# Seven probability tiles taken once and used in turn, in a fused attention and feed-forward kernel: what the writers of a tile wait for

## The chip, the cores and the metric

The kernel runs on one core of one Trainium2 chip. The time is the device time of one execution in microseconds (us); it is given as the median of three runs. Beside it stands one profiled execution, whose hardware trace is what the profile's views are made from. The engines of the core are named as the profile names them: PE (matrix products; PEld is its loading of weights), DVE (vector), ACT (activations), POOL, and SP, which issues most of the transfers.

## The reference

The input is one sequence of 2048 tokens of width 512. Two branches are computed and mixed by a gate per token.

```python
g = sigmoid((x * gate_w).sum(-1))
q = (x @ wq)  -> 32 heads of 16        k = x @ wk, v = x @ wv   # one key and value head for all
p = softmax(q k^T * 16**-0.5)
a = (p v, heads side by side) @ wo
b = (silu(x @ w_gate) * (x @ w_up)) @ w_down                    # width 1792
out = g * a + (1 - g) * b
```

## The kernel before

**Numbers.** Products are made in a fast 32-bit format; to keep accuracy each factor is split into a high and a low part and three products are added (`split`, `three`). Queries carry high and low parts in 48 rows of a 64-row half, so that a score product is one matmul of 64 rows, and two of them stand side by side in the array. The products of the projections and of the feed-forward branch ("jobs", line 198) are also cut into halves of 64 rows; PE runs a lower half of one job beside the upper half of an earlier one.

**Attention.** Keys lie on the 128 partitions. For head h and key tile kt (16 of them), numbered together u = 16 h + kt, `score(u, j)` makes the scores of 128 keys against 1024 queries (j = 0 or 1) in a PSUM tile `pss` of two banks (line 741, two matmuls). There are two `pss` buffers, so a score product needs the one that the score product two before it used. `exps` turns scores into probabilities on ACT (line 749), into the probability tile `pt[u]`, 128 x 2048 numbers. There are two kinds of score tile. Kind A: ACT takes all 1024 columns out of PSUM. Kind H, "half": ACT takes the first 512 columns, DVE copies the other 512 raw into `pt` (line 745), and ACT makes their exponentials later in place (line 749, `pt<-pt`). `mix(u)` multiplies `pt[u]` by the values and by a column of ones (line 761, `po`), 32 rows at a time, four products side by side.

**Blocks.** After a first stage (u below 32, in pairs, all of kind A, with the last projections of the queries between), the rest runs in 120 blocks of four key tiles. A table writes the order out by hand: `STEPS` = "SSFFFFFSFSFFFSFFFSFFFFSS" (S a score product, F a step of feed-forward work on PE), then the four `mix`. `KINDS` = "AHHAAHHA" names the kinds of the eight score tiles of a block, here called tile 0 to tile 7, and `EXPS` = "0d 1d 2d 3d 4d 5d 5s 1s 2s | 6d T 7d 6s" is ACT's order (d straight from PSUM, s in place, T a tanh of the feed-forward branch). The first of the 120 blocks has all tiles of kind A, the last one has fewer tiles.

**Probability tiles.** `new_pt(u)` takes a new `pt` tile for each u: three buffers (`PTB`) lie in one pool, four (`PTL`) in another that opens when the query weights are gone; from u = 33 on they are used in turn, so that a buffer comes back after seven key tiles. The framework that turns the program into instructions finds for each writer of a new tile who wrote and read the buffer's old content, and adds a wait for each engine whose work the writer's engine hasn't yet waited for. A wait is for a semaphore of the other engine, or of the engine itself. Where an instruction has one wait, it carries it; where it has two, the first is put into an instruction of its own, EVENT_SEMAPHORE, on the queue ahead of it.

`ACTS`, `DEFER`, `LATER` and `COPY` are lists of feed-forward and normalisation work for ACT and DVE, which the blocks hand out between the attention steps.

Of the kernel before, what the change touches and what calls it, by code (L numbers as in the profile page):

```python
# [8 lines left out]
F32 = mybir.dt.float32  # L9
# [9 lines left out]
P = 128  # L19
S = 2048  # L20
D = 512
H = 32
DH = 16
F = 1792
KD = D // P
NT = S // P
CH = 512
# [20 lines left out]
PTB = 3  # L48
# [3 lines left out]
PTL = 4  # L52
# [13 lines left out]
def tile_gated_mix(ctx, tc, x, wq, wk, wv, wo, w_gate, w_up, w_down, gate_w, out):  # L66
    nc = tc.nc
# [19 lines left out]
    vaug = cpool.tile([P, NT, 2 * DH], F32, name="vaug")  # L87
# [18 lines left out]
    ACC, PAIR = {}, []  # L106
# [21 lines left out]
    def run(queue, n):  # L128
        for _ in range(min(n, len(queue))):
            queue.pop(0)()  # L130
# [592 lines left out]
    with tc.tile_pool(name="bpool", bufs=2) as bp:  # L723
        PT = {}
# [2 lines left out]
            nc.sync.dma_start(new_qs(h).bitcast(F32), q_d[h])  # L727


        def new_pt(u):  # L730
            late = u > 2 * BEGIN and (u - 2 * BEGIN) % (PTB + PTL) >= PTB
            PT[u] = (PAIR[1] if late else bp).tile([P, S], F32, name="pt", bufs=PTL if late else PTB)

        def score(u, j, half=False):
            h, kt = divmod(u, NT)
            if j == 0:
                new_pt(u)
            ps = ps_s.tile([P, 2 * CH], F32, name="pss")
            for b in range(2):
                rows = slice(b * RT, (b + 1) * RT)  # L740
                nc.tensor.matmul(ps[:, b * CH:(b + 1) * CH], ks[rows, kt * P:(kt + 1) * P], QS[h][rows, j, :],  # L741
                                 start=True, stop=True)
            halves.clock += 1
            pt = PT[u][:, j * 2 * CH:(j + 1) * 2 * CH]
            other = nc.vector.tensor_copy(pt[:, CH:], ps[:, CH:]) if half else None  # L745
            return pt, ps, other

        def exps(pt, ps, other=None, w=slice(None)):
            ins = nc.scalar.activation(pt[:, w], ps[:, w], AF.Exp, scale=SCALE)  # L749
            if other is not None:  # L750
                tc.declare_no_dep(getattr(ins, "ins", ins), getattr(other, "ins", other), reason="another bank")

        def mix(u):
            h, kt = divmod(u, NT)
            pt = PT.pop(u)
            if kt == 0:
                run(COPY, 1)
                PO[:] = [ps_o.tile([P, CH], F32, name="po")]
            po = PO[0]
            for c in range(NCH):  # L760
                nc.tensor.matmul(po[c * 2 * DH:(c + 1) * 2 * DH, :], vaug[:, kt, :], pt[:, c * CH:(c + 1) * CH],  # L761
                                 start=(kt == 0), stop=(kt == NT - 1))
            if kt == NT - 1:

                osb = hp.tile([P, CH], F32, name="osb")
                rsb = hp.tile([P, CH], F32, name="rsb", bufs=1)

                def invert(i):
                    w = slice(i * P, (i + 1) * P)
                    nc.vector.reciprocal(rsb[:, w], rsb[:, w])  # L770

                def store():
                    nc.vector.tensor_tensor(osb, osb, rsb, ALU.mult)
                    for c in range(NCH):
                        nc.sync.dma_start(o_d[h * DH:(h + 1) * DH, c * CH:(c + 1) * CH],
                                          osb[c * 2 * DH:c * 2 * DH + DH, :])

                assert not LATER
                COPY.append(lambda: nc.vector.tensor_copy(osb, po))
                LATER.extend([(0.8, lambda: nc.vector.stream_shuffle(rsb, osb, [DH] * 2 * DH))] +  # L780
                             [(1.0, lambda i=i: invert(i)) for i in range(TC)] + [(0.8, store)])

        NU = H * NT
        SPANS, u = [], 2 * BEGIN
# [6 lines left out]
        def feed(k, more=True):  # L791
            for _ in range(k):
                if JOBS or halves.busy():
                    halves.step(more)

        def block(k, u0, size, first, last, steps, kinds, order):
            more = k < NB - STOP
            tiles = [(u, j) for u in range(first, last) for j in range(2)]
            order = list(order)
            made = []  # L800

            def emit():
                while order and order[0] != "|" and (order[0] == "T" or int(order[0][:-1]) < len(made)):
                    what = order.pop(0)
                    if what == "T":
                        run(ACTS, len(ACTS))
                        continue
                    i, how = int(what[:-1]), what[-1]
                    pt, ps, other = made[i]
                    if how == "s":  # L810
                        exps(pt, pt, w=slice(CH, None))
                    else:
                        exps(pt, ps, other, slice(0, CH) if kinds[i] == "H" else slice(None))

            for i, what in enumerate(steps):
                if what == "F":
                    if "S" in steps[i + 1:i + 3] and kinds[len(made):len(made) + 1] == "H":
                        HOLD.append(i)
                    feed(1, more)
                    HOLD.clear()  # L820
                elif len(made) < len(tiles):
                    made.append(score(*tiles[len(made)], kinds[len(made)] == "H"))
                    emit()
                    run(EVAC, len(EVAC))
                if len(made) > 4:
                    run(COPY, 1)
            if order:
                order.pop(0)
            run(ACTS, len(ACTS))
            emit()  # L830
            assert not order and len(made) == len(tiles)
            left = BUDGET * size / 4
            rest = len([v for v, _ in SPANS if v >= u0 and v // NT == u0 // NT])
            for _ in range(max(-(-len(LATER) // rest), 0 if DEFER else 2)):
                if LATER:
                    cost, f = LATER.pop(0)
                    left -= cost
                    f()
            for last in (False, True):
                kept = set()  # L840
                for item in list(DEFER):
                    n, cost, f = item
                    if n in kept or (n in FRESH) != last or cost > left:
                        kept.add(n)
                    else:
                        DEFER.remove(item)
                        left -= cost
                        f()
            FRESH.clear()
            for u in range(u0, u0 + size):  # L850
                mix(u)
            halves.clock += size * LONG // 2
# [7 lines left out]
        with tc.manual_schedule():  # L860
            for j in range(2):
                exps(*score(0, j))
            for n in range(BEGIN):
                quota = RATE
                u = 2 * n
                if n == 0:
                    feed(FIRST)
                exps(*score(u + 1, 0))
                if n == 0:
                    feed(quota - FIRST)  # L870
                exps(*score(u + 1, 1))
                feed(FIRST)
                exps(*score(u + 2, 0))
                feed(quota - FIRST)
                exps(*score(u + 2, 1))
                settle()
                mix(u)
                mix(u + 1)
                halves.clock += LONG
                run(COPY, 1)  # L880
                if LATER:
                    LATER.pop(0)[1]()
                if n == NT // 2 + 1:
                    load_head(2)
# [62 lines left out]
    with tc.If(rv != 0):  # L947
        with tc.tile_pool(name="gpool", bufs=2) as gp:
            with tc.For_i(0, H, 1) as h:
# [4 lines left out]
                for qt in range(NT):  # L954
# [3 lines left out]
                    for half in range(2):  # L958
                        ps = ps_s.tile([P, 2 * CH], F32, name="pss")
                        for j in range(2):  # L960
                            c = half * 2 + j
# [9 lines left out]
                    po = ps_o.tile([P, CH], F32, name="po")  # L971
                    for b in range(NT // TC):
                        pt = ps_f.tile([P, CH], F32, name="pf")
                        for i in range(TC):
                            kt = b * TC + i
# [3 lines left out]
                        for i in range(TC):  # L979
                            kt = b * TC + i  # L980
                            nc.tensor.matmul(po[:2 * DH, :P], vaug[:, kt, :], ptc[:, i * P:(i + 1) * P],
                                             start=(kt == 0), stop=(kt == NT - 1))
# [39 lines left out]
```

## Time and profile before

| | |
|---|---|
| median of three runs | 1346.02 us (1345.85 to 1346.98) |
| the profiled execution's own time | 1346.55 us |
| its span in the profile | 1344.5 us |
| busy in the span | PE 1331.0 us, ACT 1088.3, DVE 786.8, weight loads 779.0, POOL 225.1 |
| granted PE clock | 0.998 of full speed |

The span is the time from the first to the last instruction of the program in the trace; 2 us of the execution lie outside it. PE's busy time is a union of instructions whose ends are modelled, so a PE that is busy 99% may still lose time inside: what it loses is seen in the distance from the start of one matmul to the start of the next, in the view of the instructions in order of time.

### The profile page before, as it was taken

The numbers are of one execution on the slowest core, as the hardware profiler recorded it, in microseconds if no ns is written. First come the engines' busy times: TensorE is split into PE (matmuls) and PEld (weight loads), VectorE is DVE, ScalarE is ACT, GpSimd is POOL, SyncE is SP. The second block draws the span as 40 slices with busy tenths as digits, with TensorE's granted clock in tenths as the row PEclk, the third lists the DMA queues.
The fourth block names the chain that finished last, engine by engine and source line by source line (L and its number), as shares of the span: only waits on it lengthen the run. The fifth ranks groups of instructions, "written<-read, shape, count | busy, mean of one in ns | idle before, by whom it ended". The sixth has DMA issues, their size and how long they took to land.

```text
span 1344.5 us, 27205 instructions
## 1 busy us (share of the span) xinstructions
PE 1331.0 (99%) x10782; PEld 779.0 (58%) x10782; DVE 786.8 (59%) x1342; ACT 1088.3 (81%) x1596; POOL 225.1 (17%) x229
## 2 busy tenths in 40 slices
PE   9999999999999999999999999999999999999988
PEld 7655555555555555555555555555555555555677
DVE  4654566566565665666556666565555666566542
ACT  4578898889898888889888889888888889888501
POOL 6250231142141151142010000000000000001043
PEclk9999999999999999999999999999999999999999
DMA  8676021131144372263234342242231342242254
GB/s 285 210 241 218 20 65 41 40 98 36 52 129 141 107 240 91 68 218 104 83 123 146 121 136 68 67 154 76 65 107 62 127 130 66 68 161 91 83 191 151
DMA packets 102515, 157.35 MB, mean 117 GB/s; under 512 B 11888, under 2 KB 43376, under 8 KB 100720
## 3 DMA queue, kind: packets, MB, share of 16 engines
q1 hardware_dynamic: 100656, 155.36, 35.9%
q8 instruction: 88, 1.44, 0.5%
q10 hardware_dynamic: 1728, 0.20, 0.1%
q14 instruction: 43, 0.35, 0.1%
HBM read 99.42 MB, written 55.57 MB: 115 GB/s over the span
## 4 chain that ended last, share of the span: by engine, by line
PE 97%; DVE 2%; ACT 1%; issue 0%; DVEq 0%; ACTq 0%
PE pf L198 37%; PE po L761 34%; PE pss L741 21%; PE pf L120 4%; PE pss L627 0%; ACT pt L749 0%; DVE rsb L770 0%; PE po L614 0%; DVE hl L111 0%; DVE hh L110 0%; DVE xl L632 0%; PE pss L667 0%; DVE rsb L780 0%; DVE ht L337 0%; DVE pt L745 0%
## 5 line engine op out<-in xcount | busy, mean ns | idle before, releaser
L749 ACT ACTIVATE pt<-pss 128x1024 f32<-128x1024 f32 (+1 forms) x1024 | 783.0, 823 | 144.5 <-PE pss L741 125.3
L745 DVE COPY pt<-pss 128x512 f32<-128x512 f32 x475 | 328.1, 691 | 396.1 <-PE pss L741 391.6
L761 PE MATMUL po<-pt,vaug 128*32 128x512 f32 x4096 | 468.0, 595 | 0.0
L741 PE MATMUL pss<-qs,ks 64*128 64x512 f32 x2048 | 404.0, 423 | 1.4 <-DVE sign L484 1.0
L741 PEld LDWEIGHTS pss<-qs,ks 64*128 64x128 f32 x2048 | 192.4, 184 | 217.4 <-ACT pt L749 189.1
L749 ACT ACTIVATE pt<-pt 128x512 f32<-128x512 f32 x475 | 272.7, 621 | 17.5 <-DVE pt L745 10.7
L761 PEld LDWEIGHTS po<-pt,vaug 128*32 128x32 f32 x4096 | 131.3, 109 | 246.4 <-issue 222.3
L198 PE MATMUL pf<-xh,wgh 64*128 64x512 f32 (+1 forms) x444 | 164.9, 391 | 0.0
L198 PE MATMUL pf<-xh,wgl 64*128 64x512 f32 (+1 forms) x444 | 164.7, 390 | 0.0
L198 PE MATMUL pf<-xl,wgh 64*128 64x512 f32 (+1 forms) x444 | 164.2, 390 | 0.0
L198 PE MATMUL pf<-xh,wul 64*128 64x512 f32 (+1 forms) x440 | 160.7, 390 | 0.0
L198 PE MATMUL pf<-xh,wuh 64*128 64x512 f32 (+1 forms) x440 | 160.5, 390 | 0.1
L198 PE MATMUL pf<-xl,wuh 64*128 64x512 f32 (+1 forms) x440 | 160.1, 390 | 0.0
L198 PE MATMUL pf<-wdh,hh 64*128 64x512 f32 x416 | 136.2, 390 | 0.0
L198 PE MATMUL pf<-wdl,hh 64*128 64x512 f32 x416 | 135.0, 390 | 0.0
L198 PE MATMUL pf<-wdh,hl 64*128 64x512 f32 x416 | 134.6, 390 | 0.0
L770 DVE RECIPROCAL rsb<-rsb 128x128 f32<-128x128 f32 x128 | 116.7, 933 | 1.8 <-issue 0.8
L515 POOL CAST xh<-wraw 128x512 fp32r<-128x512 f32 x4 | 2.9, 727 | 513.2 <-DMA wraw<-o_d 513.2
L198 PEld LDWEIGHTS pf<-xl,wgh 64*128 64x128 f32 (+1 forms) x444 | 80.4, 185 | 8.2 <-issue 0.8
L198 PEld LDWEIGHTS pf<-xh,wgl 64*128 64x128 f32 (+1 forms) x444 | 80.6, 185 | 7.7
L198 PEld LDWEIGHTS pf<-xh,wgh 64*128 64x128 f32 (+1 forms) x444 | 80.3, 185 | 8.0 <-issue 0.5
L198 PEld LDWEIGHTS pf<-xh,wuh 64*128 64x128 f32 (+1 forms) x440 | 78.5, 185 | 8.4 <-issue 0.6
(170 smaller groups left out, 1384.6 us busy)
## 6 DMA issues: line engine op xcount, KB each, us to landing
qs<-q_d SPq DMA_DIRECT2D x31, 512.0 KB, 4.9
q_d<-hh SPq DMA_DIRECT2D x28, 256.0 KB, 3.8
wraw<-in_B_w_gate_dram SPq DMA_DIRECT2D x28, 256.0 KB, 3.7
wraw<-in_B_w_up_dram SPq DMA_DIRECT2D x28, 256.0 KB, 3.1
wraw<-in_B_w_down_dram SPq DMA_DIRECT2D x28, 256.0 KB, 3.2
wgh<-w_d SPq DMA_DIRECT2D x28, 256.0 KB, 2.7
wgl<-w_d SPq DMA_DIRECT2D x28, 256.0 KB, 2.9
wuh<-w_d SPq DMA_DIRECT2D x28, 256.0 KB, 2.7
```

The lines of the kernel that those rows point to most:

```text
L120: nc.tensor.matmul(ps, a, b, start=(i == 0), stop=(i == n - 1))
L198: ins = nc.tensor.matmul(self.ps, a, b, start=(i == 0 and opens), stop=(last and closes))
L515: nc.gpsimd.tensor_copy(OT[c][0][:, k, :], raw)
L741: nc.tensor.matmul(ps[:, b * CH:(b + 1) * CH], ks[rows, kt * P:(kt + 1) * P], QS[h][rows, j, :], start=True, stop=True)
L745: other = nc.vector.tensor_copy(pt[:, CH:], ps[:, CH:]) if half else None
L749: ins = nc.scalar.activation(pt[:, w], ps[:, w], AF.Exp, scale=SCALE)
L761: nc.tensor.matmul(po[c * 2 * DH:(c + 1) * 2 * DH, :], vaug[:, kt, :], pt[:, c * CH:(c + 1) * CH], start=(kt == 0), stop=(kt == NT - 1))
L770: nc.vector.reciprocal(rsb[:, w], rsb[:, w])
```

## The change

Each of the seven buffers gets one `pt` tile (`HOME`), taken at its first use and handed out again for every later key tile of that buffer. Since the framework now sees one tile that is written again and again, it would find its old writers and readers by itself; the new code tells it which of these to leave out (`settled`, "ordered by others"): a writer of the first kind (exponentials from PSUM, DVE's copy) doesn't wait for the old writers of the tile, the exponential in place doesn't wait for the old readers, and `mix` doesn't wait for DVE's copies, which the exponential in place has waited for. What is left for a writer from PSUM is the wait for its score product.

```diff
--- before.py
+++ after.py
@@ -727,9 +727,28 @@
             nc.sync.dma_start(new_qs(h).bitcast(F32), q_d[h])
 
 
+        SLOT, HOME, PAST, USED, OLD = {}, {}, {}, {}, {}
+
         def new_pt(u):
             late = u > 2 * BEGIN and (u - 2 * BEGIN) % (PTB + PTL) >= PTB
-            PT[u] = (PAIR[1] if late else bp).tile([P, S], F32, name="pt", bufs=PTL if late else PTB)
+            SLOT[late] = SLOT.get(late, -1) + 1
+            slot = (late, SLOT[late] % (PTL if late else PTB))
+            if slot not in HOME:
+                HOME[slot] = (PAIR[1] if late else bp).tile([P, S], F32, name="pt", bufs=PTL if late else PTB)
+            PT[u] = HOME[slot]
+            OLD[u] = {kind: [ins for used in PAST.get(slot, []) for ins in used[kind]]
+                      for kind in ("write", "copy", "read")}
+            USED[u] = {"write": [], "copy": [], "read": []}
+            PAST[slot] = PAST.get(slot, [])[-8:] + [USED[u]]
+
+        def settled(ins, others):
+            for other in others:
+                tc.declare_no_dep(getattr(ins, "ins", ins), getattr(other, "ins", other), reason="ordered by others")
+
+        def wrote(u, ins, kind="write"):
+            if OLD[u]:
+                settled(ins, OLD[u]["write"] + OLD[u]["copy"])
+            USED[u][kind].append(ins)
 
         def score(u, j, half=False):
             h, kt = divmod(u, NT)
@@ -742,13 +761,20 @@
                                  start=True, stop=True)
             halves.clock += 1
             pt = PT[u][:, j * 2 * CH:(j + 1) * 2 * CH]
-            other = nc.vector.tensor_copy(pt[:, CH:], ps[:, CH:]) if half else None
-            return pt, ps, other
-
-        def exps(pt, ps, other=None, w=slice(None)):
+            other = None
+            if half:
+                other = nc.vector.tensor_copy(pt[:, CH:], ps[:, CH:])
+                wrote(u, other, "copy")
+            return pt, ps, other, u
+
+        def exps(pt, ps, other, u, w=slice(None)):
             ins = nc.scalar.activation(pt[:, w], ps[:, w], AF.Exp, scale=SCALE)
-            if other is not None:
-                tc.declare_no_dep(getattr(ins, "ins", ins), getattr(other, "ins", other), reason="another bank")
+            if pt is ps:
+                if OLD[u]:
+                    settled(ins, OLD[u]["read"])
+            elif other is not None:
+                settled(ins, [other])
+            wrote(u, ins)
 
         def mix(u):
             h, kt = divmod(u, NT)
@@ -758,8 +784,10 @@
                 PO[:] = [ps_o.tile([P, CH], F32, name="po")]
             po = PO[0]
             for c in range(NCH):
-                nc.tensor.matmul(po[c * 2 * DH:(c + 1) * 2 * DH, :], vaug[:, kt, :], pt[:, c * CH:(c + 1) * CH],
-                                 start=(kt == 0), stop=(kt == NT - 1))
+                ins = nc.tensor.matmul(po[c * 2 * DH:(c + 1) * 2 * DH, :], vaug[:, kt, :],
+                                       pt[:, c * CH:(c + 1) * CH], start=(kt == 0), stop=(kt == NT - 1))
+                settled(ins, USED[u]["copy"])
+                USED[u]["read"].append(ins)
             if kt == NT - 1:
 
                 osb = hp.tile([P, CH], F32, name="osb")
@@ -806,11 +834,11 @@
                         run(ACTS, len(ACTS))
                         continue
                     i, how = int(what[:-1]), what[-1]
-                    pt, ps, other = made[i]
+                    pt, ps, other, u = made[i]
                     if how == "s":
-                        exps(pt, pt, w=slice(CH, None))
+                        exps(pt, pt, None, u, slice(CH, None))
                     else:
-                        exps(pt, ps, other, slice(0, CH) if kinds[i] == "H" else slice(None))
+                        exps(pt, ps, other, u, slice(0, CH) if kinds[i] == "H" else slice(None))
 
             for i, what in enumerate(steps):
                 if what == "F":
```

The instructions of each engine and their order are the same in both programs; the memory addresses of the seven tiles too. What differs is what the instructions wait for. On ACT, in one block (rows of the instruction order with the semaphores waited for; PE_49, DVE_49 and Activation_49 are those of PE, DVE and ACT), the rows from tile 0's exponential to the in-place exponential of tile 6 read before:

```order
L749 ACTIVATE pt<-pss 128x1024 [waits PE_49,Activation_49]
L749 ACTIVATE pt<-pss 128x512 [waits PE_49] x2
L749 ACTIVATE pt<-pss 128x1024 [waits PE_49]
L749 ACTIVATE pt<-pss 128x1024 [waits PE_49,Activation_49]
L749 ACTIVATE pt<-pss 128x512 [waits PE_49]
L749 ACTIVATE pt<-pt 128x512 [waits DVE_49]
L749 ACTIVATE pt<-pt 128x512 x2
L319 ACTIVATE hs<-hs 128x512 [waits DVE_49]
L749 ACTIVATE pt<-pss 128x512 [waits PE_49]
L749 ACTIVATE pt<-pss 128x1024 [waits PE_49]
L749 ACTIVATE pt<-pt 128x512 [waits DVE_49]
```

and now:

```order
L771 ACTIVATE pt<-pss 128x1024 [waits PE_49]
L771 ACTIVATE pt<-pss 128x512 [waits PE_49] x2
L771 ACTIVATE pt<-pss 128x1024 [waits PE_49] x2
L771 ACTIVATE pt<-pss 128x512 [waits PE_49]
L771 ACTIVATE pt<-pt 128x512 [waits DVE_49]
L771 ACTIVATE pt<-pt 128x512 x2
L319 ACTIVATE hs<-hs 128x512 [waits DVE_49,Activation_49]
L771 ACTIVATE pt<-pss 128x512 [waits PE_49]
L771 ACTIVATE pt<-pss 128x1024 [waits PE_49]
L771 ACTIVATE pt<-pt 128x512 [waits DVE_49]
```

Tiles 0 and 4 no longer wait for ACT's own earlier work, and no EVENT_SEMAPHORE stands ahead of them; over the program 269 exponentials lose that wait, and nine tanhs of line 319 gain one. On DVE, in the same block, from the copy of tile 1 to the first work after the copy of tile 6, before:

```order
L745 COPY pt<-pss 128x512 [waits PE_49]
L305 COPY hs<-pf 128x512 [waits PE_49]
L745 COPY pt<-pss 128x512 [waits PE_49]
L484 MEMSET sign 1x1 [waits PE_49]
L745 COPY pt<-pss 128x512 [waits PE_49,Activation_49]
L335 TENSOR_TENSOR ht<-hs,pf 128x512 [waits DVE_49,PE_49]
L745 COPY pt<-pss 128x512 [waits PE_49,Activation_49]
L773 TENSOR_TENSOR osb<-osb,rsb 128x512
```

and now:

```order
L766 COPY pt<-pss 128x512 [waits PE_49]
L305 COPY hs<-pf 128x512 [waits PE_49]
L766 COPY pt<-pss 128x512 [waits PE_49]
L484 MEMSET sign 1x1 [waits PE_49]
L766 COPY pt<-pss 128x512 [waits PE_49]
L335 TENSOR_TENSOR ht<-hs,pf 128x512 [waits DVE_49,PE_49]
L766 COPY pt<-pss 128x512 [waits PE_49]
L801 TENSOR_TENSOR osb<-osb,rsb 128x512
```

The copies of tiles 5 and 6 lose their wait for ACT. Such waits stand in some blocks and not in others: of the 475 copies 158 had one, and all 158 lose it. By place in the block these are 66 copies of tile 5, 65 of tile 6 and 27 of tile 1; no copy of tile 2 had one. On PE, POOL and SP no wait differs.

## The prediction

> **What bounds the kernel now.** I read the page first, then the list of waits, then the instructions of single blocks in order of time. On the page, the busy times and the chain of work that ended last:
>
> ```profile
> PE 1331.0 (99%) x10782; PEld 779.0 (58%) x10782; DVE 786.8 (59%) x1342; ACT 1088.3 (81%) x1596; POOL 225.1 (17%) x229
> ...
> PE 97%; DVE 2%; ACT 1%; issue 0%; DVEq 0%; ACTq 0%
> ```
>
> PE sets the end, so only what PE loses counts. Its "99%" hides losses, since matmuls overlap and their ends are modelled. The list of waits (engine, line, who released it: total, times, longest) says where to look:
>
> ```profile
> PEld pss L741 <- ACT pt L749: 189.1, 490, 1.4
> ACT pt L749 <- PE pss L741: 125.3, 138, 2.8
> DVE pt L745 <- PE pss L741: 391.6, 393, 3.9
> ```
>
> PE's weight loads for score products wait for exponentials, and the exponentials at a block's start and DVE's copies wait for scores: a ring through the two `pss` buffers. Idle time of the weight load is not yet lost time of PE, so I went through one block's PE rows (start, duration, count), from tile 0's score to tile 4's:
>
> ```profile
> 613.93 0.73 PE L741 MATMUL pss<-qs,ks 64*128 64x512 f32 x4
> ...
> 615.40 0.39 PE L198 MATMUL pf<-xl,wgh 64*128 64x512 f32 x1
> ...
> 615.62 0.48 PE L741 MATMUL pss<-qs,ks 64*128 64x512 f32 x2
> 615.94 0.40 PE L198 MATMUL pf<-xh,wgl 64*128 64x512 f32 x1
> ...
> 616.18 0.42 PE L741 MATMUL pss<-qs,ks 64*128 64x512 f32 x2
> 616.43 0.39 PE L198 MATMUL pf<-wdh,hh 64*128 64x512 f32 x1
> ...
> 617.12 0.40 PE L741 MATMUL pss<-qs,ks 64*128 64x512 f32 x2
> 617.36 0.39 PE L198 MATMUL pf<-wdh,hh 64*128 64x512 f32 x1
> ```
>
> A step of two matmuls side by side takes 0.22 to 0.24 from start to start (615.40 to 615.62, 617.12 to 617.36). Tile 2's score takes 0.32 and tile 3's 0.25. The other place that loses is the end of a block, tiles 6 and 7 and then the first `mix`:
>
> ```profile
> 609.78 0.65 PE L741 MATMUL pss<-qs,ks 64*128 64x512 f32 x4
> 610.36 0.64 PE L761 MATMUL po<-pt,vaug 128*32 128x512 f32 x4
> ...
> 619.22 0.70 PE L741 MATMUL pss<-qs,ks 64*128 64x512 f32 x4
> 619.85 0.64 PE L761 MATMUL po<-pt,vaug 128*32 128x512 f32 x4
> ```
>
> The same two steps take 0.58 in one block and 0.63 in the next. Of the 118 like blocks, 102 have all their matmul records, the first from 148.37 us and the last from 1248.73. Their rows (first and last block: tile 2's score and what follows; tiles 6 and 7 and what follows):
>
> ```profile
> 150.09 0.47 PE L741 MATMUL pss<-qs,ks 64*128 64x512 f32 x2
> 150.39 0.40 PE L198 MATMUL pf<-xl,wuh 64*128 64x512 f32 x2
> ...
> 153.65 0.64 PE L741 MATMUL pss<-qs,ks 64*128 64x512 f32 x4
> 154.22 0.64 PE L761 MATMUL po<-pt,vaug 128*32 128x512 f32 x4
> ...
> 1250.44 0.47 PE L741 MATMUL pss<-qs,ks 64*128 64x512 f32 x2
> 1250.75 0.40 PE L198 MATMUL pf<-wdl,hh 64*128 64x512 f32 x2
> ...
> 1253.99 0.71 PE L741 MATMUL pss<-qs,ks 64*128 64x512 f32 x4
> 1254.64 0.64 PE L761 MATMUL po<-pt,vaug 128*32 128x512 f32 x4
> ```
>
> Over the 102, tile 2's step takes 0.309 on average, 0.082 above the 0.227 of an undisturbed step; tile 3's is 0.028 above; tile 7's takes 0.341 where the copy of tile 5 had no separate wait (43 blocks) and 0.407 where it had one (59). All other steps stand at their least time in nearly every block; a mean block takes 9.486. So there is some 0.15 per block to be had at most, and I ask how much of it hangs on the waits removed.
>
> **The change, part by part.** Removed are waits that stood alone on the queues (queue, count, duration):
>
> ```profile
> L749 ACTq EVENT_SEMAPHORE  x276: 17/17/8380, 40.2 to 1261.8; - x138
> L745 DVEq EVENT_SEMAPHORE  x159: 21/21/21, 139.8 to 1262.8; - x159
> ```
>
> What was waited for lay some 20 ACT instructions back and was long done. What costs is the extra instruction between the score's arrival and the work. ACT's starts in the block above, tile 0's score first, then its exponential (with a separate wait), and tile 2's (without), whose score ran from 615.62 for 0.48:
>
> ```profile
> 613.93 0.50 PE L741 MATMUL pss<-qs,ks 64*128 64x512 f32 x2
> ...
> 614.53 1.03 ACT L749 ACTIVATE pt<-pss 128x1024 f32<-128x1024 f32 x1 [1.14 <-PE pss L741]
> ...
> 616.14 0.60 ACT L749 ACTIVATE pt<-pss 128x512 f32<-128x512 f32 x1
> ```
>
> ACT begins 0.10 after the score's end with the wait (614.43 to 614.53) and 0.04 without (616.10 to 616.14); over the 102 blocks 0.104 against 0.033. For DVE, tile 5's score and copy, without the wait and with it:
>
> ```profile
> 608.62 0.42 PE L741 MATMUL pss<-qs,ks 64*128 64x512 f32 x2
> ...
> 609.08 0.69 DVE L745 COPY pt<-pss 128x512 f32<-128x512 f32 x1 [0.72 <-PE pss L741]
> ...
> 618.06 0.40 PE L741 MATMUL pss<-qs,ks 64*128 64x512 f32 x2
> ...
> 618.59 0.69 DVE L745 COPY pt<-pss 128x512 f32<-128x512 f32 x1 [1.72 <-PE pss L741]
> ```
>
> From the score's start 0.46 and 0.53; over the blocks, 0.065 and 0.131 after its end. Both engines give a price of 0.07 per separate wait that stands before an idle engine.
>
> Term 1, tile 0. Its exponential frees the buffer that tile 2's score needs:
>
> ```profile
> 615.61 0.19 PEld L741 LDWEIGHTS pss<-qs,ks 64*128 64x128 f32 x2 [0.25 <-ACT pt L749]
> ```
>
> ACT's exponential ends at 615.56, the load starts at 615.61, 0.01 before its matmul is due, and the load of the step behind it is late in turn. In the 102 blocks a score's load, however late, is followed by the next step's matmul 0.333 later, so a step loses what its load's lead lacks of 0.106. With tile 0 begun 0.068 earlier, tile 2's lead of 0.024 becomes 0.092, and the loss of 0.082 becomes 0.014. What is late next is tile 3's score: it needs tile 1's exponential, which follows tile 0's on ACT and moves with it, while PE arrives earlier by the same amount, so its 0.028 stays. Bounds per block: nothing below, 0.082 above; I take 0.068, the price itself, since the step lacks more than that. 118 x 0.068 = 8.0 us.
>
> Tile 4's wait goes too, but tiles 5 to 7's scores stood at their least time behind it, so it is worth nothing on PE.
>
> Term 2, tile 5. DVE's copy frees the buffer of tile 7's score. The natural experiment is in the trace: 0.407 against 0.341, so 0.066 in each of the 66 blocks whose copy of tile 5 loses the wait: 4.4 us. Bounds: 0 and 0.066, since the 43 blocks without it show no rest to win. The 65 waits at tile 6 and the 27 at tile 1 free buffers whose next score comes a `mix` later or waits for ACT longer: nothing.
>
> Term 3, the first stage: 16 pairs of key tiles, in which the fourth score's step is 0.045 above the 0.337 that the change to `mix` takes otherwise:
>
> ```profile
> 102.10 0.45 PE L741 MATMUL pss<-qs,ks 64*128 64x512 f32 x2
> 102.48 1.92 PE L761 MATMUL po<-pt,vaug 128*32 128x512 f32 x16
> ```
>
> Here 0.38. It waits for the second exponential, which follows the first, and that had a separate wait: 16 x 0.045 = 0.7 us, at least nothing.
>
> The nine waits that line 319 gains cost ACT 9 x 0.07 = 0.6 us; ACT sits idle 1.14 before the next block's first score in the row of 614.53, so they are hidden, and 0.6 is their price without that cover. One tile per buffer instead of many adds no instruction, and addresses and order are the same.
>
> Sum: 8.0 + 4.4 + 0.7 = 13.1 us. The profiled execution took 1346.55 (span 1344.5), so it becomes 1333.45 (span 1331.4). The median lies 0.53 below it: 1332.9 us.
>
> The Trainium skill, VectorE: DVE Perf Modes, section "The DRAIN you can't avoid", reports eight copies with a semaphore after each taking as long as eight with one after the last, so that the semaphore costs nothing extra. Read as a rule for waits, it would make the change worth nothing and leave 1346.0; the copies above, 0.07 later with a separate wait than without, speak against it here, since they start on an idle engine and not in a stream.
>
> **The rivals.**
>
> *A. Only DVE's part arrives.* Tile 0 follows a `mix`, and its lag of 0.10 could be the array's return to score products and not the wait. For it: tile 0 is the one tile that always has the wait, so no block shows it without. Against: tile 4, whose score (617.12 for 0.40, above) has no `mix` ahead, has the wait and starts 0.10 after its score as well:
>
> ```profile
> 617.62 1.51 ACT L749 ACTIVATE pt<-pss 128x1024 f32<-128x1024 f32 x2
> ```
>
> Then 1346.0 - 4.4 = 1341.6.
>
> *B. Only ACT's part arrives,* if DVE's copy waits for something else in those 66 blocks: 1346.0 - 8.7 = 1337.3. Against: the two kinds of block differ in this step alone.
>
> *C. Nothing.* A satisfied wait costs nothing because the queue hides it, or the framework puts other waits in place of those named: 1346.0. Against: the instruction order shows none but the nine, and the rows show the 0.07.
>
> *D. Slower.* DVE's copy and ACT's exponential of one tile now start closer together, and both read the same `pss` tile and write the same `pt`. If they slowed each other by more than the 0.07 gained, PE's next score would be later. It decides where a copy takes more than 0.76 or tile 0's exponential more than 1.10. At 0.1 beyond that, in the 118 blocks at tile 2, it costs 11.8 us: 1358. Against: 0.69 for the copies in both blocks above.
>
> *E. More.* The loss left at tile 2 and tile 3 goes as well, because tile 1 ends early enough: a further 118 x (0.014 + 0.028) = 5.0 us, so 1327.9. Against: tile 1's exponential starts when tile 0's ends.
>
> **How the numbers follow.** The forecast has 0.77, A 0.06, B 0.05, C 0.05, D 0.03, E 0.04. The time is 1332.9. Its own range, with the price at 0.06 to 0.075 and term 3 from 0 to 0.7, is 1331.5 to 1335.5. To hold 8 in 10 and B, which lies nearest, it reaches up to 1338.0, and down to 1330.0 for half of E. Differences below 0.2% (2.7 us) can't be told from none here. Faster by more than that are the forecast, A, B and E: 0.92; same is C: 0.05; slower is D: 0.03.
>
> **What would show it.** In the profile after: hardly any EVENT_SEMAPHORE at the exponential's and the copy's lines; tile 0's exponential about 0.035 after its score's end; tile 2's step at 0.24 (0.31 now), tile 3's still 0.25, tile 7's 0.34 in every block, a block at about 9.38. If tile 2's step stays at 0.31 though ACT starts earlier, term 1 is wrong; if tile 0's lag stays at 0.10, A holds; if tile 3's step grows, the ring has merely moved its loss there. A copy or exponential that takes longer speaks for D.

## The result, and the profile after

Five runs of the changed kernel took 1335.54 us in the median (1333.84 to 1337.81), five of the kernel before 1346.76 (1345.85 to 1350.85): a ratio of 0.9913, with a 95% interval of 0.9893 to 0.9933. The change makes the kernel faster, by 0.9%, and the time lies in the range predicted, 2.6 us above the 1332.9 named. Timed again beside other kernels, the same program took 1334.41 (five runs, 1333.31 to 1335.12). The execution profiled after the change took 1335.54, its span is 1333.4.

On the page after: the busy times, and the group of all score matmuls with its busy time and the mean duration of one; the last line is that group before:

```profile
PE 1320.8 (99%) x10782; PEld 777.8 (58%) x10782; DVE 788.2 (59%) x1342; ACT 1082.8 (81%) x1596; POOL 224.4 (17%) x229
...
L760 PE MATMUL pss<-qs,ks 64*128 64x512 f32 x2048 | 390.7, 412 | 0.7 <-ACT pt L771 0.4
...
L741 PE MATMUL pss<-qs,ks 64*128 64x512 f32 x2048 | 404.0, 423 | 1.4 <-DVE sign L484 1.0
```

PE's busy time falls by 10.2 us and the score matmuls' by 13.3, although not one instruction was taken from them. Time lost to a late weight load counts as busy in them: in the block before, tile 2's matmuls begin at 615.62 by their records, while their weights load from 615.61 to 615.80, and the two take 0.48; in the block after they take 0.41. That is the loss that the page's 99% hid.

The waiting instructions at the lines of the exponential and of the copy, and two of the waits:

```profile
L771 ACTq EVENT_SEMAPHORE  x7: 17/38/8380, 41.6 to 132.5; - x7
L766 DVEq EVENT_SEMAPHORE  x1: 21/21/21, 140.4 to 140.4; - x1
...
PEld pss L760 <- ACT pt L771: 161.4, 394, 0.8
ACT pt L771 <- PE pss L760: 116.5, 139, 2.8
```

276 and 159 have become 7 and 1. The weight loads wait 161.4 us for exponentials, not 189.1, and 394 times, not 490. The block shown before (from 613.93 us), now:

```profile
609.46 0.73 PE L760 MATMUL pss<-qs,ks 64*128 64x512 f32 x4
...
611.16 0.41 PE L760 MATMUL pss<-qs,ks 64*128 64x512 f32 x2
611.41 0.40 PE L198 MATMUL pf<-xh,wgl 64*128 64x512 f32 x1
...
611.65 0.41 PE L760 MATMUL pss<-qs,ks 64*128 64x512 f32 x2
611.90 0.39 PE L198 MATMUL pf<-wdh,hh 64*128 64x512 f32 x1
...
614.67 0.65 PE L760 MATMUL pss<-qs,ks 64*128 64x512 f32 x4
615.25 0.64 PE L787 MATMUL po<-pt,vaug 128*32 128x512 f32 x4
```

Tile 2's step takes 0.25 (0.32 before), tile 3's 0.25 as before, and tiles 6 and 7 together 0.58 (0.63). ACT's and DVE's rows of the same block, with tile 0's score by itself:

```profile
609.46 0.50 PE L760 MATMUL pss<-qs,ks 64*128 64x512 f32 x2
...
610.00 3.13 ACT L771 ACTIVATE pt<-pss 128x1024 f32<-128x1024 f32 x4 [1.09 <-PE pss L760]
...
613.99 0.69 DVE L766 COPY pt<-pss 128x512 f32<-128x512 f32 x1 [1.65 <-PE pss L760]
```

Tile 0's exponential starts 0.04 after its score ends at 609.96; it was 0.10. Tile 5's copy starts 0.066 after its score on average, where it was 0.131 in the blocks with the wait. Over 102 blocks with full records (before, after): tile 0's lag 0.104, 0.043; tile 2's step 0.309, 0.246; tile 3's 0.255, 0.254; tile 7's 0.380, 0.343; a mean block 9.486, 9.387 (median 9.486, 9.375).

By stages, from the starts of the matmuls: the stretch from the first block to the last `mix` took 1138.21 before and takes 1126.47, 11.7 us less. The pairs of the first stage go from 4.878 to 4.828 each, 0.75 less over these 15. The tail is the same (77.57, 77.62). What leads up to the first of the 15 pairs counted here takes 1.36 longer (it starts at 55.57 before and at 56.93 after). That stretch has no `pt` in it until its end, and the clock granted there differs. Two windows after, one before (the number ahead of the DMA share is the clock):

```profile
0.00:30.00 30.00, 26.97 (x178) 23.05 (x179) 14.35 (x25) 13.21 (x19) 15.97 (x21) 0.94 0.80 282
30.00:56.00 26.00, 26.00 (x143) 20.14 (x146) 18.74 (x32) 10.74 (x17) 11.31 (x11) 1.00 0.57 168
```

```profile
0.00:56.00 56.00, 52.71 (x328) 42.58 (x330) 32.83 (x57) 24.39 (x35) 27.20 (x31) 1.00 0.73 238
```

In the second profile of the same program the clock was 1.00 there, that pair starts at 55.77, and the span is 1331.4. So most of the 1.36 us belongs to that execution, not to the change. That 1331.4 is also the span that the sum gave is partly luck: the profile before has stalls of 1.4 us in two blocks, of a kind that comes and goes (see the end), and this one has none.

### The profile page after: what moved, and what is told of

Same layout as the page of the kernel before. It is cut to its first block, busy times and chain, and to the rows that moved or that the text cites. A ratio compares the mean times of both kernels' runs of the same rounds, so it can differ in the third digit from the quotient of the medians.

```text
span 1333.4 us, 26787 instructions
## 1 busy us (share of the span) xinstructions
PE 1320.8 (99%) x10782; PEld 777.8 (58%) x10782; DVE 788.2 (59%) x1342; ACT 1082.8 (81%) x1596; POOL 224.4 (17%) x229
## 3 DMA queue, kind: packets, MB, share of 16 engines
HBM read 99.42 MB, written 55.57 MB: 116 GB/s over the span
## 4 chain that ended last, share of the span: by engine, by line
PE 97%; DVE 2%; ACT 0%; issue 0%; DVEq 0%; ACTq 0%
PE pf L198 38%; PE po L787 34%; PE pss L760 20%; PE pf L120 4%; PE pss L627 0%; DVE rsb L798 0%; ACT pt L771 0%; PE po L614 0%; DVE hl L111 0%; DVE hh L110 0%; DVE xl L632 0%; DVE ht L323 0%; PE pss L667 0%; DVE rsb L808 0%; DVE ht L333 0%
## 5 line engine op out<-in xcount | busy, mean ns | idle before, releaser
L760 PE MATMUL pss<-qs,ks 64*128 64x512 f32 x2048 | 390.7, 412 | 0.7 <-ACT pt L771 0.4
L760 PEld LDWEIGHTS pss<-qs,ks 64*128 64x128 f32 x2048 | 191.6, 184 | 205.3 <-ACT pt L771 161.4
```

## The experiments

The theory: a wait that stands alone on a queue costs some 0.07 us between the score's arrival and the work, at every such exponential and copy, but PE pays only at two places of a block, where it waits for just that work next. Rivals were that only one engine's waits mattered, that each wait costs the end its price, and that waiting for the engine's own work is what costs. All runs are variants of the changed kernel; times are medians, to be held against its 1334.41 and 1335.54. In the diffs, which are cut to the lines that matter, `i` is the tile's place in its block.

**Tile 0's wait put back.**

```diff
-            if OLD[u]:
+            if OLD[u] and not (i == 0 if kind == "write" else False):
                 settled(ins, OLD[u]["write"] + OLD[u]["copy"])
```

> The changed kernel with one class of wait put back: the exponential of tile 0 of each block (119 of them) waits again for ACT's own old work. Theory (the separate wait instruction between the score's arrival and an idle ACT costs 0.06, and PE pays it at tile 2's score): tile 0's lag after its score back from 0.043 to 0.10, tile 2's step from 0.246 to 0.31, a block from 9.375 to about 9.44, the execution 7 to 8 us longer than the changed kernel. Rival (the lag is the array's return from mix to scores, and DVE's waits made the gain): lag and step stay, the time is that of the changed kernel.

1341.46 us (1339.84 to 1342.93). The block's rows, tile 0's score and exponential and tile 2's step:

```profile
611.95 0.50 PE L761 MATMUL pss<-qs,ks 64*128 64x512 f32 x2
...
612.55 1.03 ACT L773 ACTIVATE pt<-pss 128x1024 f32<-128x1024 f32 x1 [1.15 <-PE pss L761]
...
613.65 0.47 PE L761 MATMUL pss<-qs,ks 64*128 64x512 f32 x2
613.96 0.39 PE L198 MATMUL pf<-xh,wgl 64*128 64x512 f32 x1
```

The lag is 0.10 and the step 0.31 again (over 102 blocks 0.101 and 0.312), and the blocks take 7.8 us longer than in the changed kernel's trace; by the medians the run is 6 to 7 longer. The rival that saw the array's return from `mix` in the 0.10 falls: with the wait gone the lag is that of the other tiles, with the wait back it is back.

**Tile 4's wait put back,** with `i == 4` in the same line.

> The changed kernel with the wait put back at tile 4's exponential alone (119 waits). Theory: ACT starts tile 4 0.06 later (0.044 to 0.10 after its score), but tile 6's score, which needs that buffer, has more lead than it needs, so every PE step stays and the time is that of the changed kernel within 1 us. Rival (each such wait costs its 0.06 on ACT, and ACT's time reaches the end): 7 us longer.

1333.60 us (1332.78 to 1334.42), the changed kernel's time. Tile 4's score, and the exponentials of tiles 3 and 4, then tiles 6 and 7:

```profile
611.34 0.40 PE L761 MATMUL pss<-qs,ks 64*128 64x512 f32 x2
...
610.86 2.01 ACT L773 ACTIVATE pt<-pss 128x1024 f32<-128x1024 f32 x2
...
613.43 0.64 PE L761 MATMUL pss<-qs,ks 64*128 64x512 f32 x4
614.00 0.64 PE L789 MATMUL po<-pt,vaug 128*32 128x512 f32 x4
```

ACT pays: the pair of exponentials ends at 612.87, and with 1.03 for the second, tile 4's starts at 611.84, 0.10 after its score's end at 611.74; over the blocks 0.104, against 0.044 without the wait. PE doesn't: tiles 6 and 7 take 0.57. The same number of waits that cost 6 to 7 us at tile 0 costs nothing here.

**The wait at tile 5's copy put back,** by `not (False if kind == "write" else i == 5)`.

> The changed kernel with DVE's wait put back at the copies of tile 5 (66 of them, in the blocks that had it). Theory: in these blocks tile 7's step goes from 0.34 back to 0.41, the others stay; 4.3 us longer than the changed kernel. Rival (tile 0's wait made all of the gain, since tile 7's step is set by what ACT does): the same time as the changed kernel.

1340.51 us (1339.71 to 1341.11): 5 to 6 us longer, where 4.3 were expected. Tile 5's copy, then tiles 6 and 7 and the first `mix`:

```profile
615.36 0.69 DVE L767 COPY pt<-pss 128x512 f32<-128x512 f32 x1 [1.73 <-ACT pt L773]
...
615.96 0.73 PE L761 MATMUL pss<-qs,ks 64*128 64x512 f32 x4
616.62 0.64 PE L789 MATMUL po<-pt,vaug 128*32 128x512 f32 x4
```

The two steps take 0.66. Tile 7's step is 0.412 in the 59 blocks with the wait and 0.345 in the 43 without: 0.067, as before the change, which gives 66 x 0.067 = 4.4 us. The blocks in the trace take 6.0 longer than in the changed kernel's. Of this, the mean step of tile 7, 0.041 longer, makes 118 x 0.041 = 4.8, and the step behind tile 2's score 118 x 0.0076 = 0.9, by two stalls that come and go from run to run (below); a stall of 0.34 at tile 6's score in one block, near 364 us, is the rest. The mechanism stands; its sum is 1 to 2 us short of the medians, and that the other executions had such stalls too isn't shown. The row shows a trap too: the trace names ACT as the releaser, though the buffer's last exponential, tile 7's of two blocks before, lay 17 or 18 ACT instructions back in the 58 blocks counted. ACT's semaphore ticks with nearly each of its instructions, and the releaser is inferred from the last tick.

**The waits at the copies of tiles 6 and 1 put back,** by `not (False if kind == "write" else i in (1, 6))`.

> The changed kernel with DVE's wait put back at the copies of tiles 6 and 1 (65 and 27). Theory: each of these copies starts 0.07 later, but tile 0's score of the next block and tile 3's score wait for something later; the time is that of the changed kernel within 1 us. Rival (every wait costs its 0.07): 92 x 0.07 = 6.4 us longer.

1334.60 us (1334.48 to 1337.73): the changed kernel's time, as the theory has it. The waits are there (93 separate instructions at the copy's line, not 1), and tile 6's copy starts 0.124 after its score on average, not 0.095. 92 waits that nobody waits for are free.

**Tile 0's wait kept, but carried earlier.** The dependence is put back as in the first run, and the in-place exponential of tile 6 in the block before is made to wait for the same work, so that ACT has seen it when tile 0 comes (`follow(a, b)` makes a wait for b).

```diff
+                if u > 2 * BEGIN and (u - 2 * BEGIN) % 4 == 0 and USED.get(u - 6) and USED[u - 6]["write"]:
+                    follow(ins, USED[u - 6]["write"][-1])
```

> Tile 0's dependence on the old work is kept, as in the run that puts the wait back at tile 0, but the in-place exponential of tile 6 in the block before waits for it, 118 waits at a place where ACT has idle time behind it. Theory (it is the place that costs, not the wait): tile 0's lag stays at 0.043, tile 2's step at 0.246, the time is that of the changed kernel within 1 us. Rival (ACT's waiting for its own earlier work costs wherever it stands, as the order of its pipeline): 7 us longer, as with the wait at tile 0.

1334.53 us (1333.00 to 1336.72). The waits are on the queue, and tile 0 starts at once (its score, its exponential, tile 2's step):

```profile
L773 ACTq EVENT_SEMAPHORE  x116: 17/17/8380, 39.9 to 1242.5; - x116
...
607.41 0.50 PE L761 MATMUL pss<-qs,ks 64*128 64x512 f32 x2
607.95 1.03 ACT L773 ACTIVATE pt<-pss 128x1024 f32<-128x1024 f32 x1 [1.09 <-PE pss L761]
...
609.11 0.42 PE L761 MATMUL pss<-qs,ks 64*128 64x512 f32 x2
609.36 0.39 PE L198 MATMUL pf<-xh,wgl 64*128 64x512 f32 x1
```

So the whole gain at tile 0 is to be had with the dependence left in. What costs is the place of the waiting instruction, and no dropped dependence is needed for it.

**A third wait at tile 0.** Beside the wait for ACT's old work, the exponential follows DVE's latest work (the last low half split off or reciprocal taken). The instruction ahead takes two waits, so there is still one of it.

```diff
+            if pt is not ps and j == 0 and u > 2 * BEGIN and (u - 2 * BEGIN - 1) % 4 == 0 and LASTV:
+                follow(ins, LASTV[-1])
```

> As the run that puts tile 0's wait back, with a third wait, for DVE's latest work, which is long done by then (107 of the blocks). The instruction ahead of the exponential takes two waits, so there is still one such instruction. Theory (the price is that of the instruction, not of a wait): tile 0's lag 0.10, tile 2's step 0.31, 1341 us as with two waits. Rival (each wait that is checked costs about 0.06): lag 0.16, tile 2's step 0.37, 1348 us.

1341.41 us (1340.60 to 1344.43), the same as with two waits. In the block of these rows the lag is 0.08 (612.72 to 612.80), in most others 0.09. The last line counts the separate instructions (number, shortest, median and longest duration in ns):

```profile
612.22 0.50 PE L765 MATMUL pss<-qs,ks 64*128 64x512 f32 x2
612.80 1.03 ACT L777 ACTIVATE pt<-pss 128x1024 f32<-128x1024 f32 x1 [1.13 <-PE pss L765]
...
L777 ACTq EVENT_SEMAPHORE  x127: 17/1635/8380, 40.1 to 1251.8; - x127
```

127 of them, against 126 with two waits: a third wait adds no instruction and no 0.06. DVE's work was not always done, though. In four of 100 blocks the exponential starts 0.26 to 2.15 after its score, and PE loses 0.1 to 2.0 one step before tile 2's score; in the longest, near 591 us, it waited for a DVE subtraction of 1.66 us. These four are the main reason why the profile's mean block, 9.458, lies above its median of 9.426, and they offset a mean tile 2 step of 0.300, shorter than with two waits. So the equal times are in part a coincidence; what speaks against the rival is the usual lag, 0.09 and not 0.16.

**Which of the waits stands alone.** The trace's records of the semaphores settle a point that the prediction left open. At all 269 exponentials and 158 copies that had a separate instruction before the change, it is the wait for PE's score that stands alone; the old ACT work is waited for by the exponential or the copy itself. In the block of 614.53 the score ends at 614.43, the separate instruction runs from 614.467 to 614.484, and the exponential starts 0.045 later. So the instruction runs after the arrival, and its time is added. The same trace has the other order as well: 16 DVE instructions (12 of line 533, 4 of line 333) with a separate instruction that waited for older work and was over before PE's signal came. From that signal to the start these take 0.024 to 0.026 us, like the work with one wait (0.023 to 0.026), where the copies with the score's wait set apart take 0.091 or more, and the exponentials 0.080 or more against 0.023. All 13 profiles have these 16 or more, and the same times. A separate instruction as such is free there; it costs where it holds the wait that ends last. No run exchanges the two waits at the exponentials and copies, so that this alone would bring the gain is not shown.

**One tile per buffer, nothing declared settled.** Only the pair that the kernel before declares (copy and exponential of one tile) stays.

```diff
-            for other in others:
+            for other in []:
                 tc.declare_no_dep(...)
...
-                settled(ins, [other])
+                tc.declare_no_dep(..., reason="another bank")
```

> The seven tiles taken once, as in the changed kernel, but nothing is declared settled (beside the pair of DVE's copy and ACT's exponential of one tile, as in the kernel before): 420 exponentials and 185 copies wait for ACT's old work, among them tile 0 in every block and tile 5 in 66. Theory: as before, tile 2's step 0.31, tile 7's 0.41 in the 66 blocks, 1345 to 1347 us. Rival (one tile per buffer is itself the gain): the time of the changed kernel, 1333 to 1336.

1347.75 us (1346.41 to 1348.59), a ratio of 1.0013 (1.0003 to 1.0022) to the kernel before. The waits on the queues, and, in a late block, tile 2's step:

```profile
L771 ACTq EVENT_SEMAPHORE  x427: 17/17/8380, 39.7 to 1262.2; - x143
L766 DVEq EVENT_SEMAPHORE  x186: 21/21/21, 139.2 to 1263.2; - x186
...
1250.76 0.47 PE L760 MATMUL pss<-qs,ks 64*128 64x512 f32 x2
1251.07 0.40 PE L198 MATMUL pf<-wdl,hh 64*128 64x512 f32 x2
```

More waits than before, 427 and 186, and nearly the same time, since those at tile 0 and tile 5 are the same. The new ones at the copies of tile 2 cost a little: tile 4's score, which needs that buffer, takes a step of 0.267 in the blocks that have the wait and 0.232 in the others, or 27 x 0.035 = 0.9 us. Taking the tiles once brings nothing by itself; it is what lets the code name the old instructions.

**Two tries for the loss that is left** (0.019 at tile 2 and 0.027 at tile 3). First the kinds of tiles 0 and 1 exchanged, so that tile 0's exponential is the short one:

```diff
-KINDS = ("AHHAAHHA",)
-EXPS = ("0d 1d 2d 3d 4d 5d 5s 1s 2s | 6d T 7d 6s",)
+KINDS = ("HAHAAHHA",)
+EXPS = ("0d 1d 2d 3d 4d 5d 5s 0s 2s | 6d T 7d 6s",)
```

> The changed kernel with the kinds of tiles 0 and 1 exchanged (tile 0 half, tile 1 whole). Theory (what is left of tile 2's loss is the end of tile 0's exponential, now 0.59 long and not 1.03): tile 2's step from 0.246 to 0.228; tile 1 ends as late as before, so tile 3's step stays at 0.254; 118 x 0.018 = 2 us less than the changed kernel. Rival (DVE's copy of tile 0, 0.69 long, takes the exponential's place as the last release): tile 2's step unchanged or longer, no gain.

> Tiles 0 and 1 exchanged, once more with five rounds beside the changed kernel. Theory: 1 to 2 us less than the changed kernel, by tile 2's step of 0.235 against 0.246; rival: no difference that can be told.

1332.74 us (1332.34 to 1333.37) and, with the changed kernel on the same chip, 1333.54 (1333.21 to 1334.62) against 1334.41 (1333.31 to 1335.12): the ranges overlap. Tile 2's step falls from 0.246 to 0.235 and 0.234, but the median of the step ahead of it grows from 0.227 to 0.237 (its mean, 0.245, holds a stall of 0.8): most of what the exchange won moved one step forward. The kernel with tiles 0 and 1 exchanged can't be told from the changed kernel.

Then, with that, tile 3's score one feed-forward step later (`STEPS` "SSFFFFFSFFSFFSFFFSFFFFSS"):

> As the run with tiles 0 and 1 exchanged, and tile 3's score one feed-forward step later. Theory: tile 3's load gets 0.227 more lead, so its step goes from 0.254 to about 0.23; with the exchange a block loses 0.04 less, 118 x 0.045 = 5 us less than the changed kernel. Rival (the later tile 3 delays ACT's tiles 3 to 5 by 0.2, and tile 7's score, which waits for tile 5, pays): tile 7's step longer than 0.34 and no gain.

1334.62 us (1332.85 to 1336.86), no gain. Tile 3's step does fall to 0.236, and the median block to 9.351, but the mean block is 9.390: in eight blocks the step behind tile 4's score takes 0.41 to 0.66, where PE's work waits for a small DVE instruction that orders the two halves of a job, as here:

```profile
374.51 0.50 PE L760 MATMUL pss<-qs,ks 64*128 64x512 f32 x2
375.16 0.47 PE L198 MATMUL pf<-xh,wuh 64*128 64x512 f32 x1 [0.16 <-DVE sign L484]
```

A step of 0.65. The rival's delay of ACT did come (tile 4's exponential starts 0.26 after its score, not 0.04), but tile 7 didn't pay for it: its step stayed at 0.339. Part of the loss moved to a third place that neither theory had.

## Why the prediction was right, point by point

- **What bounds the kernel.** Right: PE's steps at tiles 2, 3 and 7 held the loss, nothing else moved.
- **The price of a separate wait, 0.07.** Shown by putting it back: 0.058 to 0.061 at tiles 0 and 4 on ACT, 0.077 at tile 5 on DVE. The prediction's 0.068 for ACT isn't worked out there; its rows give 0.071, from tile 2's lag of 0.033, but tile 0's own lag without the wait is 0.043. Its picture of the wait was incomplete too: the wait that stood alone was the one for the score, not the one for the old work. That is why the instruction ran after the arrival at all.
- **Term 1, 8.0 us.** Measured by the steps 118 x 0.063 = 7.4, by the run with the wait back 6 to 8. The size was off by that 0.01 of the lag.
- **Term 2, 4.4 us.** By the mean step of tile 7, 118 x 0.0365 = 4.3; putting the waits back cost 1 to 2 us more than that.
- **Term 3, 0.7 us.** 16 x 0.050 = 0.8. No run puts these waits back alone.
- **What was costed at nothing.** Tile 4's, tile 6's and tile 1's waits: two runs with them back take the changed kernel's time. Tile 3's step stayed, at 0.254.
- **The total.** 13.1 us predicted, 11.1 in the two profiled spans, 11.2 between the medians of the result, 12.0 between the medians 1346.45 and 1334.41, taken side by side. The difference in the profiles is the 1.36 us before the first pair, at a clock of 0.94 in the first 30 us, and 0.7 in terms 1 and 2. The forecast's own range is summed wrongly at its upper end: 0.06 at 118 and 66 places is 11.0 us less, so 1335.0 and not 1335.5. The 1335.54 measured lies just above either; it is inside the range that was widened for rival B.
- **The rule of the Trainium skill** (VectorE: DVE Perf Modes, "The DRAIN you can't avoid"), that a semaphore costs nothing extra, was measured on copies in a stream with a semaphore after each. It doesn't carry over to a wait that needs an instruction of its own and ends last: 0.06 on ACT, also at tile 4, where ACT works without a pause, and 0.07 on DVE.
- **The rivals.** The time alone doesn't part the forecast (1332.9) from B (1337.3), since 1335.54 lies between; the steps and the runs do. A and B each got their own run and fall: tile 0 and tile 5 both pay. C falls with the result, though its reason, a satisfied wait that costs nothing, holds for the 16 DVE instructions above. For D, the copies take 0.69 as before. E didn't happen by itself, and the two tries for it gave nothing that can be told.

## What to carry to other kernels

An instruction with two waits puts an extra one on its queue. Where that one holds the wait that ends last, it cost 0.06 to 0.08 us here after the last arrival, even if the other wait was over long ago; where it held only older waits, ahead of an idle DVE, it cost nothing. So see which wait stands alone. The price matters only where another engine waits for just that instruction, so look for the step that loses, and take the second wait away there or let an earlier instruction of the same queue, one with slack behind it, wait for it. A busy share of 99% on PE doesn't show such losses; the distance from one matmul's start to the next does, and blocks that differ in one wait are an experiment that the trace has already made.

## What the runs showed beyond that

- The step of PE behind tile 2's or tile 3's score starts 0.333 us (medians 0.333 to 0.335) after that score's weight load, before and after. An undisturbed step takes 0.227, so a lead of more than 0.106 hides the load, and each ns below it is a ns lost.
- Two blocks, near 495 and 590 us, stall for 0.1 to 1.4 us in the step behind tile 2's score or the one ahead of it in some executions and not in others, with the changed waits and without. In the longer stall of the profile before, DVE's `hl<-ht,hh` takes 1.67 us at 594.74, where most take 0.69, tile 1's copy comes after it, and tile 3's score waits for that buffer; why it takes so long is open. These stalls and the clock of the first 30 us (0.94 in one execution, 1.00 in another) make up most of the 2.0 us between the spans of the two profiles of the changed program. That they are also behind the 2 to 4 us by which the other executions of one program differ is likely, but not shown.
